# Retention and a gated convolution in one kernel: the first four phases in another order

## The chip, the cores and the metric

The kernel runs on one core of one Trainium2 chip. The metric is the time of one execution on the device, in microseconds; the median of five runs before the change is 165.16 us (164.12 to 170.69).

## What is computed

Eight batches of 576 tokens with eight heads of 64. Retention is attention without a softmax: scores are scaled, multiplied by a decay `gamma_h ** (i - j)` for `i >= j` and by zero otherwise, and multiplied with the values. Its output, 512 features per token, goes through a causal convolution over five tokens (one weight per feature and tap) whose sigmoid gates a linear layer, and through a second linear layer.

```python
scores = (1 / sqrt(64)) * q @ k.T                      # per batch and head
gamma  = 1 - 2.0 ** (-5 - arange(8))
ret    = (scores * where(rel >= 0, gamma ** rel, 0)) @ v
x      = ret.transpose(0, 2, 1, 3).reshape(8, 576, 512)
gate   = sigmoid(sum(conv_w[k] * shift(x, 4 - k) for k in range(5)))
out    = (gate * (x @ w_val)) @ w_out
```

## The kernel before, in words

**Chunks.** A sequence of 576 tokens is cut into two chunks of 256 and a tail of 64. The tails of four batches make one chunk. So there are 18 chunks m (the list `dcs`), worked off in the loop `for m in range(1, ND + 1)` (L507), with chunk 0 done in the straight code ahead of it. Round m works on chunk m's retention, on chunk m−1's convolution and values, and on projections of chunks further back. Engines take their instructions in the order in which the program issues them, since the schedule is written by hand; what an instruction waits for follows from the tiles that it reads and writes.

**Loads.** SP's queue loads k, q and v in float32, chunk by chunk (`load`, L98), the first chunk whole, later ones in two halves each. After chunk 2 comes `w_val` (1 MB), after chunk 3 `w_out` (1 MB, four pieces).

**Casts.** `cast_k`, `cast_q` make bfloat16 tiles `kb` and `qb`, each in two halves (`kb<-fk`, L224), and `cast_v` multiplies the values with the decay `gin` (L238). They run on GpSimd (POOL), except the first keys, which VectorE (DVE) casts.

**Retention of one chunk.** The keys and the queries are turned by TensorE (PE), eight transposes each (`turn`, L260), and copied out of PSUM to `kq` (`take_turned`, L268, ScalarE unless said otherwise). The target of a turn is `tps`, a pool of one bank, unless a bank of the pool `g` is passed. `scores` (L250, `s<-kq`) has two parts, r = 0 and 1, each followed by two `masks` on VectorE (L291). `values` (L305) multiplies the masked scores with the values, `carried` (L305, `o<-kq,sd`) adds what earlier tokens bring through the state. The state of a batch is accumulated in PSUM by `update(m, 0)` and `update(m, 1)` (`st<-vb,kb`), and after each half ScalarE copies it (`take_state`, L375, `sd` or `sl`); the next half writes the same bank and so waits for that copy. `take_x` (VectorE, L340) scales the result by `gout` into `x`.

**Gated layer.** `conv` (L250, `g<-x,dg`) runs the five taps as matmuls with diagonal weights `dg`, in two lists `lo` and `hi` of ten steps of two matmuls each, one list for each of two PSUM banks of the pool `g`. `gate` (ScalarE, L404) takes the sigmoid and frees a bank; `value` (L411) multiplies with `wvb`, the cast of `w_val`, and VectorE makes `z` (L414). `project` (L421) multiplies with `wob`, the cast of `w_out`; ScalarE copies the result (L429, `ob`) and SP stores it.

**Start.** ScalarE computes the tables of decay factors `gout` (four Exps of 128x576) and `gin`, then loads Sigmoid's table by a small activation (L464). VectorE and POOL make the diagonals (`prep_diagonals`, L209). `keep_warm(n)` issues n matmuls on zeros (L446), 128x512 each, which only keep TensorE active.

**Order in the rounds up to m = 3** (`late = m < 4`): eight steps of `lo` and `hi`, `update(m, 0)` between the last steps of `hi`, the state's copy, `update(m, 1)` between the last steps of `lo`, the copy, then `carried(m, 1)` and `scores(m, 1)`. Then keys of chunk m+1 are turned, except that round 2 does so after its two `value` calls; then come `value` and `project` calls by a small table, casts of chunk m+2, `values(m)`, `take_x(m)`, the turn of the queries (round 1 does it before `values`), and a second table of `value` and `project` calls.

Of the kernel before, what the change touches and what calls it, by code (L numbers as in the profile page):

```python
# [13 lines left out]
F32 = mybir.dt.float32  # L14
# [7 lines left out]
def kernel(  # L22
# [58 lines left out]
    with tc.manual_schedule():  # L81
# [45 lines left out]
        def prep_wo(copy, part):  # L127
            copy(wob[:, 2 * part:2 * part + 2], wof[:, 2 * part:2 * part + 2])


        zeros = consts.tile([P, DM], BF16, name="zeros")
        nc.vector.memset(zeros, 0.0)
        ident = consts.tile([P, P], BF16, name="ident")
        nc.gpsimd.memset(ident, 1.0)
        nc.gpsimd.affine_select(ident, ident, pattern=[[-1, P]], base=0, channel_multiplier=1,
# [47 lines left out]
                                lrow.unsqueeze(1).unsqueeze(3).to_broadcast([P, NCH + 1, H, R]), op=ALU.mult)  # L183

        gout = consts.tile([P, NP, S], F32, name="gout")
        for pr in range(NP):
            nc.scalar.activation(gout[:, pr, :], posi, AF.Exp, bias=lsc, scale=lcol[:, pr:pr + 1])
            if pr == 1:
                nc.scalar.activation(gin, gin, AF.Exp)
        warm = consts.tile([P, 1], F32, name="warm")  # L190

        xg = [[xp.tile([P, GB, NP, PAD + (W if c < NCH else TAIL)], BF16, name=f"x{g}{c}") for c in range(NCH + 1)]
              for g in range(B // GB)]
# [14 lines left out]
        def prep_diagonals(o, eng, ones=None):  # L208
            eng.tensor_tensor(dg[:, o], cw[:, :, o].unsqueeze(2).to_broadcast([P, KC, HP]),  # L209
                              (id2 if ones is None else ones).unsqueeze(1).to_broadcast([P, KC, HP]), op=ALU.mult)  # L210
# [16 lines left out]
        def cast_k(m, *copies):  # L227
            cast("k", m, copies)

        def cast_q(m, *copies):  # L230
            cast("q", m, copies)
# [10 lines left out]
        def run(*lists):  # L242

            for k in range(max(map(len, lists), default=0)):
                for group in lists:
                    for f in group[k] if k < len(group) else []:
                        f()
# [6 lines left out]
        def turn(which, m, bank=None):  # L254

            src = (kbf, qbf)[which][m]
            dst = new_bank() if bank is None else bank
            for pr in range(NP):
                for r in range(R):
                    nc.tensor.transpose(dst[:, pr, r, :], src[:, pr, r, :, :].rearrange("p i d -> p (i d)"), ident)  # L260
            return dst

        def take_turned(which, m, bank, *copies):
            if m not in kq:
                kq[m] = tp_sb.tile([P, 2, NP, R, P], BF16, name="kq", bufs=2)
            o = 0
            for (copy, n) in copies or ((nc.scalar.copy, NP),):
                copy(kq[m][:, which, o:o + n], bank[:, o:o + n])  # L268
                o += n
            assert o == NP  # L270
# [86 lines left out]
        def update(m, ab):  # L357
            if m >= ND or dcs[m][0] != "full":
                return []
            kind, b, c = dcs[m]  # L360
            if b not in st:
                st[b] = ps_st.tile([P, NP, D], F32, name="st")
            return [[mm(st[b][half[i], pr, :], lhsT=kbf[m][half[ab], pr, r, i, :],
                        rhs=vbf[m][half[ab], head(pr, i), r, :],
                        start=(c == 0 and ab == 0 and pr == 0 and r == 0), stop=(c == NCH - 1 and ab == 1 and r == R - 1))
                     for r in range(R) for i in range(2)] for pr in range(NP)]
# [74 lines left out]
        def keep_warm(n, t=None):  # L441

            if t is None:
                t = ps_o.tile([P, NP, R, HP], F32, name="o0").rearrange("p o r n -> p (o r n)")
            for _ in range(n):
                nc.tensor.matmul(t, zeros[:, 0:P], zeros, start=True, stop=True)  # L446
# [4 lines left out]
        ones = ps_st.tile([P, NP, D], F32, name="st")[:, 0, :]  # L451
        nc.tensor.matmul(ones, ident, idb, start=True, stop=True)
        keep_warm(6)
        cast_k(0, (v_copy, 0), (v_copy, 1))
        prep_diagonals(0, nc.gpsimd)
        bank = turn(0, 0)
        take_turned(0, 0, bank, (v_copy, 4))
        cast_q(0)
        for o in range(1, NP):
            prep_diagonals(o, nc.vector, ones)  # L460
        keep_warm(1)
        bank = turn(1, 0, spare(ps_g, "g", [P, NP, R, P], BF16))
        take_turned(1, 0, bank)
        nc.scalar.activation(warm, lsc, AF.Sigmoid)  # L464
        cast_v(0)
        for (name, f) in (("k", cast_k), ("q", cast_q), ("v", cast_v)):
            f(1)
        keep_warm(2)
        run(scores(0, 0))
        masks(0, 0, 0)  # L470
# [1 line left out]
        run(scores(0, 1, spare=True))  # L472
        masks(0, 1, 0)
        masks(0, 1, 1)
        keep_warm(2)
        run(update(0, 0))
        take_state(0, 0)
        run(update(0, 1))
        take_state(0, 1)
        keep_warm(2)  # L480
        run(carried(0, 1))
        bank = turn(0, 1)
        take_turned(0, 1, bank, (s_copy, 1), (s_copy, 3))
        keep_warm(1)

        nc.tensor.matmul(spare(ps_g, "g")[:, 0:P], zeros[:, 0:P], kq[1][:, 0, 0, 0, :], start=True, stop=True)
        run(*values(0, 1))
# [8 lines left out]
        pass_on(0)  # L496
        cast_v(2)
        prep_wv(g_copy, 1)
        keep_warm(4, spare(ps_g, "g"))
        run(scores(1, 0))  # L500
        masks(1, 0, 0)
        masks(1, 0, 1)
# [4 lines left out]
        for m in range(1, ND + 1):  # L507
            now, nxt, last = ok(m), ok(m + 1), m == ND
            late = m < 4
            hi, lo = conv(m - 1)  # L510

            if now and m > 1:
                run(scores(m, 0))
                masks(m, 0, 0)
                masks(m, 0, 1)
            if last:
                run(lo, hi)
                gate(m - 1, 1)
                gate(m - 1, 0)
            elif late:  # L520
                run(lo[0:8], hi[0:8])
                run(pairs(update(m, 0)), hi[8:10])
                take_state(m, 0)
                gate(m - 1, 0)
                run(pairs(update(m, 1)), lo[8:10])
                take_state(m, 1)
                gate(m - 1, 1)
                run(carried(m, 1))
            else:
                run(carried(m, 1))  # L530
                run(pairs(update(m, 1)), lo[0:2])
                take_state(m, 1)
                run(lo[2:10], hi[0:8])
                gate(m - 1, 1)
                run(pairs(update(m + 1, 0)), hi[8:10])
                take_state(m + 1, 0)
                gate(m - 1, 0)
            if now:
                run(scores(m, 1))
                masks(m, 1, 0)  # L540
                masks(m, 1, 1)

            if last:
                value(m - 1, 1, spare(ps_s, "s1"))
                value(m - 1, 0, spare(ps_s, "s0"))
                project(m - 2, 0)
                project(m - 2, 1)
                project(m - 1, 0, last=True)
                project(m - 1, 1, last=True)
                continue  # L550
            def turn_keys():
                if nxt:
                    bank = turn(0, m + 1)
                    take_turned(0, m + 1, bank)

            def turn_queries():
                if nxt:
                    bank = turn(1, m + 1, spare(ps_g, "g", [P, NP, R, P], BF16) if m == 1 else None)
                    take_turned(1, m + 1, bank)

            if m != 2:
                turn_keys()
            if m == 1:
                turn_queries()
                keep_warm(4, spare(ps_g, "g"))

            if m == 2:
                prep_wv(s_copy, 0)
            for (f, n, i) in {1: (), 2: ((value, 0, 1), (value, 0, 0)),
                              3: ((value, 2, 1), (project, 0, 0), (project, 0, 1))}.get(  # L570
                                  m, ((value, m - 1, 1), (project, m - 2, 0))):
                f(n, i)
            if m == 2:
                turn_keys()
            if m == 2:
                prep_wo(g_copy, 1)
            if ok(m + 2):
                cast_k(m + 2)
                cast_q(m + 2)
                cast_v(m + 2)  # L580

            run(*values(m, 1))
            run(*values(m, 0))
            run(carried(m, 0))
            take_x(m, 0)
            take_x(m, 1)
            pass_on(m)

            if m > 1:
                turn_queries()  # L590
            if m == 1:
                keep_warm(2, spare(ps_g, "g"))
            if m == 2:
                prep_wo(s_copy, 0)
            for (f, n, i) in {1: (), 2: ((value, 1, 1), (value, 1, 0)),
                              3: ((value, 2, 0), (project, 1, 0), (project, 1, 1))}.get(
                                  m, ((value, m - 1, 0), (project, m - 2, 1))):
                f(n, i)
            for name in "kqv":
                if ok(m + 2 + LB):  # L600
                    load(name, m + 2 + LB)
            if m == 3:
                run(update(m + 1, 0))
                take_state(m + 1, 0)
# [28 lines left out]
```

## Time and profile before

| | |
|---|---|
| median of five runs | 165.16 us |
| profiled execution, whole | 164.12 us |
| its span in the profile | 162.4 us |
| ScalarE (ACT) busy | 93.2 us, 57% |
| POOL busy | 82.2 us, 51% |
| mean DMA rate over the span | 248 GB/s, 40.36 MB |

A row of the timeline reads: start and busy time in us, engine, line, operation, output <- inputs, how many, and in brackets how long the engine stood idle before it and what released it. PEld is the loading of weights, which overlaps matmuls. Matmuls of one row overlap, so the sum of their durations is more than the row's time. The ends of matmuls are modelled.

The rounds begin, by the start of their main run of convolution matmuls, at 16.16, 22.73, 32.77, 43.71 and 52.27 us (m = 1 to 5).

### The profile page before, as it was taken

To read this page: it belongs to the slowest core of one execution; us is meant where nothing else is said; L and a number is where in the kernel's file an instruction comes from. 1 tells how busy PE (TensorE), PEld (TensorE's weight loads), DVE (VectorE), ACT (ScalarE), POOL (GpSimd) and SP (SyncE) were. 2 spreads that over 40 slices of the span, in tenths; PEclk is the share of its full clock that TensorE was granted. 3 is DMA by queue.
4 is the path that set the end of the run, shared out by engine and by line. 5 is a ranking of instruction groups with operands and counts; after the bars stand their busy time and mean duration, and the time that the engine had idled before them with its cause. 6 is when DMAs were issued, how large, how long until landed. Compare 5 with 4: busy or idle time off the path is not lost.

```text
span 162.4 us, 7764 instructions
## 1 busy us (share of the span) xinstructions
PE 147.3 (91%) x3391; PEld 105.9 (65%) x3391; DVE 100.3 (62%) x186; ACT 93.2 (57%) x151; POOL 82.2 (51%) x120
## 2 busy tenths in 40 slices
PE   6978877889989999999899999998999999999970
PEld 2435756776566777777577868775777777765720
DVE  6783665765548586775467767675766767766210
ACT  3875636755564757665566657574657576652340
POOL 4597767478845432557566848364746155000000
PEclk9999999999999999999999999999999999999997
DMA  4999999999998568999999997999894777121134
GB/s 123 346 346 343 384 304 253 305 316 311 347 342 251 158 147 196 277 330 319 339 336 307 316 300 224 264 316 321 253 296 122 177 178 263 40 97 66 68 129 129
DMA packets 69729, 40.36 MB, mean 248 GB/s; under 512 B 14891, under 2 KB 64063, under 8 KB 69695
## 3 DMA queue, kind: packets, MB, share of 16 engines
q1 hardware_dynamic: 69504, 39.59, 82.0%
q8 instruction: 26, 0.43, 1.1%
q10 hardware_dynamic: 190, 0.27, 0.6%
q14 instruction: 9, 0.07, 0.1%
HBM read 30.42 MB, written 9.44 MB: 245 GB/s over the span
## 4 chain that ended last, share of the span: by engine, by line
PE 83%; ACT 6%; DMA 3%; issue 3%; DVE 1%; POOL 1%; ACTq 0%; SPq 0%
PE g L421 19%; PE g L411 18%; PE g L250 14%; PE tps L260 11%; PE o L305 8%; PE s L250 6%; PE st L250 4%; DMA fqe<-in_q_dram 3%; ACT kq L268 2%; ACT sd L375 1%; PE s L411 1%; ACT ob L429 1%; PE g L260 1%; POOL qb L224 1%; ACT gate L404 1%
## 5 line engine op out<-in xcount | busy, mean ns | idle before, releaser
L291 DVE TENSOR_TENSOR p<-s,mask 128x512 bf16<-128x512 f32 x62 | 39.9, 685 | 19.9 <-PE s L250 19.9
L268 ACT COPY kq<-tps 128x1024 bf16<-128x1024 bf16 (+2 forms) x33 | 32.6, 992 | 14.5 <-PE tps L260 14.2
L411 PE MATMUL g<-x,wvb 128*128 128x256 bf16 x272 | 35.3, 273 | 1.5 <-ACT wvb L215 0.7
L421 PE MATMUL g<-wob,z 128*128 128x512 bf16 x144 | 36.4, 379 | 0.0
L238 POOL TENSOR_TENSOR vb<-fv,gin 128x1024 bf16<-128x1024 f32 x15 | 28.5, 1902 | 12.9 <-DMA fv<-in_v_dram 12.9
L429 ACT COPY ob<-g 128x512 f32<-128x512 f32 x34 | 19.9, 586 | 25.6 <-PE g L421 24.5
L250 PE MATMUL g<-x,dg 64*64 64x256 bf16 x720 | 30.8, 272 | 1.5 <-DVE x L340 0.6
L340 DVE TENSOR_TENSOR x<-o,gout 128x512 bf16<-128x512 f32 x32 | 22.2, 745 | 15.2 <-PE o L305 15.2
L411 PEld LDWEIGHTS <-wvb 128*128 128x128 bf16 x288 | 26.6, 98 | 4.8 <-issue 1.1
L414 DVE TENSOR_TENSOR z<-gate,g 128x512 bf16<-128x512 f32 x34 | 23.4, 687 | 9.1 <-PE g L411 8.2
L404 ACT ACTIVATE gate<-g 128x512 f32<-128x512 f32 x36 | 21.3, 603 | 10.7 <-DVE p L291 5.4
L250 PEld LDWEIGHTS <-dg 64*64 64x64 bf16 x720 | 23.1, 105 | 4.4 <-issue 2.8
L224 POOL CAST kb<-fk 128x512 bf16<-128x512 f32 x30 | 17.6, 615 | 7.7 <-DMA fk<-in_k_dram 5.6
L421 PEld LDWEIGHTS <-z 128*128 128x128 bf16 x144 | 14.1, 98 | 10.6 <-issue 0.5
L224 POOL CAST qb<-fq 128x512 bf16<-128x512 f32 x30 | 17.6, 616 | 6.5 <-DMA fq<-in_q_dram 4.5
L250 PE MATMUL s<-kq 64*64 64x128 bf16 (+1 forms) x560 | 15.8, 217 | 1.2 <-ACT kq L268 0.9
L250 PEld LDWEIGHTS <-kq 64*64 64x64 bf16 x576 | 11.4, 106 | 8.3 <-issue 7.8
L353 POOL COPY x<-x 128x16 bf16<-128x16 bf16 x16 | 3.2, 197 | 24.6 <-DVE x L340 24.6
L250 PE MATMUL st<-vb,kb 64*64 64x64 bf16 x512 | 13.6, 193 | 1.9 <-ACT sd L375 1.8
L250 PEld LDWEIGHTS <-kb 64*64 64x64 bf16 x512 | 12.0, 109 | 3.5 <-issue 3.5
L305 PEld LDWEIGHTS <-vb 64*64 64x64 bf16 x576 | 8.5, 107 | 8.4 <-issue 8.3
L375 ACT CAST sd<-st 128x256 bf16<-128x256 f32 x24 | 8.9, 370 | 7.8 <-PE g L250 6.2
(75 smaller groups left out, 132.1 us busy)
## 6 DMA issues: line engine op xcount, KB each, us to landing
out_dram<-ob SPq DMA_DIRECT2D x32, 256.0 KB, 4.2
fk<-in_k_dram SPq DMA_DIRECT2D x26, 256.0 KB, 4.9
fq<-in_q_dram SPq DMA_DIRECT2D x26, 256.0 KB, 4.9
fv<-in_v_dram SPq DMA_DIRECT2D x26, 256.0 KB, 5.1
fke<-in_k_dram SPq DMA_DIRECT2D x4, 256.0 KB, 4.5
fqe<-in_q_dram SPq DMA_DIRECT2D x4, 256.0 KB, 4.5
fve<-in_v_dram SPq DMA_DIRECT2D x4, 256.0 KB, 5.1
wvf<-in_moe_w_val_dram SPq DMA_DIRECT2D x1, 1024.0 KB
```

The costliest lines, as they stand in the source:

```text
L224: copy(dst[:, i], src[:, :, 1:3] if i else src[:, :, 0::3])
L238: eng.tensor_tensor(vbf[m][:, h:h + n], loaded["v", m][:, h:h + n], g[:, h:h + n].unsqueeze(3).to_broadcast([P, n, R, D]), op=ALU.mult)
L250: return lambda: nc.tensor.matmul(*a, skip_group_check=True, **kw)
L268: copy(kq[m][:, which, o:o + n], bank[:, o:o + n])
L291: nc.vector.tensor_tensor(p[:, :, 0:n], sps[m, r][i][:, :, 0:n], mask[dcs[m][0], r].unsqueeze(1).to_broadcast([P, NP, n]), op=ALU.mult)
L305: nc.tensor.matmul(o, start=key not in opened, stop=False, skip_group_check=True, **kw)
L340: nc.vector.tensor_tensor(xg[b // GB][c][:, b % GB, :, x0:x0 + P].rearrange("p o (n r) -> p o r n", r=R), ops[m, ab], gout[:, :, t0:t0 + P ...
L404: nc.scalar.activation(t, gps[n][i], AF.Sigmoid)
L411: nc.tensor.matmul(vps[:, j, :], lhsT=wvb[:, o, 2 * i + j, :], rhs=xs(n, slice(0, P), o, PAD), start=(j == 0 and o == 0), stop=(j == 1 and ...
L414: nc.vector.tensor_tensor(z, gsb[n][i], vps, op=ALU.mult)
L421: nc.tensor.matmul(o, lhsT=zsb[n, j // 2][:, j % 2, i * P:(i + 1) * P], rhs=wob[:, j, :], start=(j == 0), stop=(j == NP - 1))
L429: nc.scalar.copy(ob, o)
```

## The change

It touches the start and rounds 1 to 3; from round 4 on each engine gets the same instructions in the same order.

At the start, a small Exp on ScalarE (`warm`) is issued as soon as the zeros exist. The four `gout` activations become calls placed one by one. ScalarE takes half of the casts of k0, q0 and k1. The turned queries of chunk 0 are copied by VectorE, and one block of diagonals goes from VectorE to POOL. Two of the calls of `keep_warm` go and four change their count: 28 matmuls on zeros become 21.

In round 1, `carried(1, 1)` and `scores(1, 1)` come before `update(1, 1)`, and the queries of chunk 2 are turned after `values(1)`. In rounds 2 and 3 `update(m, 0)` comes after three steps of each list and `update(m, 1)` at the end, with the rest of the convolution between them; the order of the two gates is turned around. In round 3 both `value(2, ·)` stand together, the cast of half of `w_out` on ScalarE moves there from round 2, and the keys of chunk 4 are turned after `project(0, ·)`, directly before the queries.

```diff
+        warm = consts.tile([P, 1], F32, name="warm")
+        nc.scalar.activation(warm, zeros[:, 0:1], AF.Exp)
...
-        for pr in range(NP):
+
+        def prep_gout(pr):
             nc.scalar.activation(gout[:, pr, :], posi, AF.Exp, bias=lsc, scale=lcol[:, pr:pr + 1])
-            if pr == 1:
-                nc.scalar.activation(gin, gin, AF.Exp)
-        warm = consts.tile([P, 1], F32, name="warm")
+
+        prep_gout(0)
+        nc.scalar.activation(gin, gin, AF.Exp)
+        prep_gout(1)
...
-        cast_k(0, (v_copy, 0), (v_copy, 1))
+        cast_k(0, (v_copy, 0), (s_copy, 1))
         prep_diagonals(0, nc.gpsimd)
+        prep_gout(2)
         bank = turn(0, 0)
+        prep_diagonals(1, nc.vector, ones)
         take_turned(0, 0, bank, (v_copy, 4))
-        cast_q(0)
-        for o in range(1, NP):
-            prep_diagonals(o, nc.vector, ones)
+        cast_q(0, (g_copy, 0), (s_copy, 1))
+        prep_gout(3)
+        nc.scalar.activation(warm, lsc, AF.Sigmoid)
+        prep_diagonals(3, nc.gpsimd)
+        prep_diagonals(2, nc.vector, ones)
         keep_warm(1)
         bank = turn(1, 0, spare(ps_g, "g", [P, NP, R, P], BF16))
-        take_turned(1, 0, bank)
-        nc.scalar.activation(warm, lsc, AF.Sigmoid)
+        take_turned(1, 0, bank, (v_copy, 4))
         cast_v(0)
-        for (name, f) in (("k", cast_k), ("q", cast_q), ("v", cast_v)):
-            f(1)
+        cast_k(1, (s_copy, 0), (g_copy, 1))
+        cast_q(1)
+        cast_v(1)
         keep_warm(2)
...
-        keep_warm(2)
+        keep_warm(1)
         run(update(0, 0))
         take_state(0, 0)
         run(update(0, 1))
         take_state(0, 1)
-        keep_warm(2)
         run(carried(0, 1))
         bank = turn(0, 1)
         take_turned(0, 1, bank, (s_copy, 1), (s_copy, 3))
-        keep_warm(1)
...
-        keep_warm(4, spare(ps_g, "g"))
+        keep_warm(2, spare(ps_g, "g"))
...
             elif late:
-                run(lo[0:8], hi[0:8])
-                run(pairs(update(m, 0)), hi[8:10])
+                n = 8 if m == 1 else 3
+                run(lo[0:n], hi[0:n])
+                run(pairs(update(m, 0)), lo[n:n + 2])
                 take_state(m, 0)
+                run(lo[n + 2:10], hi[n:8])
+                gate(m - 1, 1)
+                if m > 1:
+                    run(pairs(update(m, 1)), hi[8:10])
+                    take_state(m, 1)
+                else:
+                    run(hi[8:10])
                 gate(m - 1, 0)
-                run(pairs(update(m, 1)), lo[8:10])
-                take_state(m, 1)
-                gate(m - 1, 1)
                 run(carried(m, 1))
...
                 masks(m, 1, 1)
+            if m == 1:
+                run(pairs(update(m, 1)))
+                take_state(m, 1)
...
-            if m != 2:
+            if m not in (2, 3):
                 turn_keys()
             if m == 1:
-                turn_queries()
-                keep_warm(4, spare(ps_g, "g"))
+                keep_warm(2, spare(ps_g, "g"))
...
-                              3: ((value, 2, 1), (project, 0, 0), (project, 0, 1))}.get(
+                              3: ((value, 2, 1), (value, 2, 0))}.get(
...
-            if m > 1:
-                turn_queries()
+            if m == 3:
+                prep_wo(s_copy, 0)
+                project(0, 0)
+                project(0, 1)
+                turn_keys()
+            turn_queries()
             if m == 1:
-                keep_warm(2, spare(ps_g, "g"))
-            if m == 2:
-                prep_wo(s_copy, 0)
+                keep_warm(3, spare(ps_g, "g"))
...
-                              3: ((value, 2, 0), (project, 1, 0), (project, 1, 1))}.get(
+                              3: ((project, 1, 0), (project, 1, 1))}.get(
```

## The prediction

> **What bounds the kernel now.** I read the page's table of engines first, then its slices, then the waits of the first phases, then the timeline around each wait.
>
> ```profile
> PE 147.3 (91%) x3391; PEld 105.9 (65%) x3391; DVE 100.3 (62%) x186; ACT 93.2 (57%) x151; POOL 82.2 (51%) x120
> ...
> PE   6978877889989999999899999998999999999970
> ...
> PE 83%; ACT 6%; DMA 3%; issue 3%; DVE 1%; POOL 1%; ACTq 0%; SPq 0%
> ```
>
> TensorE binds: 91% of the span and 83% of the chain. But the slices (4.06 us each) show where it is not full: up to 36 us they stand at 6 to 8, later at 9. The change works in that stretch only. Busy time by stretch says how much is there: from 8.9 to 42.4 us TensorE is busy 28.9 of 33.5 us, so 4.6 us are idle, and 4.25 us of the busy time are matmuls on zeros (line 446), which fill waits. More than that sum, 8.9 us, cannot be won. From 51.2 to 150 us it is busy 96.5 of 98.8 us with nothing of the change in it: what the early phases win arrives at the end as it is.
>
> Who ends TensorE's waits there, from the view of waits for 8.9 to 43.5 us (us in total, times, longest):
>
> ```profile
> PE st L250 <- ACT sd L375: 1.8, 4, 0.5
> PE s L250 <- ACT kq L268: 0.9, 2, 0.7
> PE g L411 <- ACT wvb L215: 0.7, 1, 0.7
> PE g L250 <- DVE x L340: 0.6, 1, 0.6
> PE tps L260 <- ACT kq L268: 0.5, 1, 0.5
> ```
>
> It is ScalarE, not a load, that TensorE waits for: the second half of a state update behind the copy of the state, scores behind the copy of turned keys and queries. The timeline has the pieces (start us, us, engine):
>
> ```profile
> 2.81 1.28 ACT L187 ACT_TABLE_LOAD   x1 [2.81 <-DVE tok L164]
> 8.10 1.01 ACT L268 COPY kq<-g 128x1024 bf16<-128x1024 bf16 x1 [0.71 <-PE g L260]
> 9.13 1.28 ACT L464 ACT_TABLE_LOAD   x1
> 14.68 1.03 PE L446 MATMUL g<-zeros 128*128 128x512 bf16 x4
> 24.09 0.37 ACT L375 CAST sd<-st 128x256 bf16<-128x256 f32 x1 [2.80 <-PE g L250]
> 24.51 0.22 PE L250 MATMUL st<-vb,kb 64*64 64x64 bf16 x3 [0.45 <-ACT sd L375]
> 28.58 1.01 ACT L268 COPY kq<-tps 128x1024 bf16<-128x1024 bf16 x1 [1.64 <-PE tps L260]
> 29.64 0.61 PE L260 MATMUL tps<-ident,qb 128*128 128x128 bf16 x8 [0.47 <-ACT kq L268]
> ```
>
> The last two rows matter most later: one bank serves keys and queries, so the queries of a chunk are turned only once ScalarE has emptied the bank, 1.01 us after it begins.
>
> [...] the first Exp starts at 4.11, 0.02 us after the load ended. [...] at 29.10 one load of qb went ahead, its matmul stood until 29.64. So a waiting turn holds all matmuls behind it. [...] Here the first ten zero matmuls run about 0.43 us apart, the four at 14.68 about 0.217. [...]
>
> **Part by part.** I replay the program order of the changed kernel in the rows' durations; loads land as before.
>
> Start, to the first scores (9.16). ScalarE loads Exp's table at about 1.45, after issuing its load of conv_w, and not at 2.81. But the exp of gin must wait for VectorE's product (4.35 to 4.55), so only one gout (0.81) comes before it: gin 4.57 to 4.8, gout to 5.57, then half of the first key cast. Its cost on ScalarE is not shown; nearest rows are wvb (0.62) and ob (0.59); bounds 0.5 to 0.7, I take 0.6. The keys are ready at 6.15; two VectorE casts made it 5.97, so 0.15 worse. Queries: POOL's half lands at 6.8, ScalarE's follows a third gout (6.1 to 6.9) and ends 7.5; before 7.38. The copy of the turned queries goes to VectorE (0.69 by its row, against 1.01): 8.2 to 8.9. Scores at 8.95, so −0.2. One diagonal goes to POOL (0.91) between its half of q and the values' load, which lands at 7.84: it ends at 7.75, hidden by that wait; without that cover it costs 0.9.
>
> First chunk, to scores(1,0) (15.94). The Sigmoid table load now runs 8.25 to 9.53 and is followed by half of k1's cast (to 10.35). The first state copy then starts at 10.35, not 10.75: −0.4. Two zero matmuls between update(0,1) and carried go (0.54), one more before the turn's copy: carried 11.2 (12.08), turn of k1 to 11.9, its first copy 12.35 (13.34), masks ready 11.95. Values 12.4, turn of q1 to 13.75 (q1's cast still ends by 12.03), copy to 14.85. Scores(1,0) at 14.9: −1.04 in all. Two of four zero matmuls behind it go and gain nothing: copy kq ends the wait.
>
> m = 1, to conv(1) (22.73). The state wait stays (0.35 of 0.45, four matmuls are put into it), but carried and scores(1,1) come ahead of update(1,1): masks end 18.75 (20.06), values 18.8 (20.52), x done 20.95 (22.68). That would be −1.7. However, the queries of chunk 2 are now turned after the values: turn 19.5 to 20.1, ScalarE's copy to 21.15, scores(2,0) in front of the convolution. Conv(1) at 21.45: −1.28. The new wait is the copy, 0.45 us beyond the zero matmuls; conv(1) and all behind it queue there.
>
> m = 2, to conv(2) (32.77). update(2,1) starts behind 22 matmuls of the convolution (28 ns each, 0.6 us), which cover the state copy (0.04+0.37+0.05): −0.46. ScalarE is next late: state copy 23.8, gate 24.3, two wvb casts (1.14) to 25.4, where value(0,0) stood at 26.99. It waits 1.0 where it waited 0.7, so of 0.46 about 0.3 arrives: −1.6. The wait of the turn of q3 (0.47) stays. POOL's order is unchanged. Conv(2) at 31.2: −1.57.
>
> m = 3, to the end of project(1,1) (42.48). The state wait (0.43) is covered again: −2.0. value(2,0) comes up beside value(2,1), so its product waits for VectorE's masks (1.29), covered by the two values and values(3). The wob cast (1.05) moves from 31.20 to about 33.9 and ends at 34.95, before project(0,0) at 35.6. The turn of k4 leaves its place among other work and stands right before the turn of q4, in the one bank: turn to 38.05, ScalarE's copy (its ob copies are done by 38.1) to 39.1, then the turn of q4. **New wait, 1.05 us**, with both turns' matmuls and four products' worth of projections queued behind it; in the kernel before, 3.4 us of work stood between. project(1,1) ends at 41.5: −1.0.
>
> SP: the loads keep their order, and early loads go out without waiting for compute; the first four output stores come about 1 us earlier at most. From m = 4 the instruction order is the same.
>
> Sum of the stages: −0.2 −0.84 −0.24 −0.29 −0.43 = −2.0, and +1.05 for the new wait: about −1.0 us. The profiled execution took 164.12 (span 162.4 and 1.72 around it), so it would be 163.1. That run was the lowest of five; the median is 165.16, so I forecast **164.2**, −0.6%. A measurement of this kernel can tell about 1%, 1.65 us, from no change.
>
> **Rivals.** (a) The sum and its unknowns, −0.3 to −1.65: 163.5 to 164.9. The unknown ScalarE cast (±0.1, twice) and the chain's pauses shown as "issue" (four of 0.5 to 0.72, with no releaser, which may fall elsewhere) make its width. Chance 0.5.
>
> (b) The pair of turns costs little, or the waits that zero matmuls hide are shorter than I take them: without the new wait −2.05, 163.1; with one "issue" pause halved too (−0.25) 162.9. For it: TensorE has up to 8.9 us to give. Against it: only one bank, and the 0.47 wait at 29.64 shows the mechanism. Chance 0.28.
>
> (c) The change does not speed what it says, since loads bind: DMA is full until 48 us and POOL waits for v1, q2, wvf, v3. Against: before, v1's cast ended 14.27 and is wanted at 15.9, q2's 17.88 at 19.5, wvf's 21.93 at 23.5, v3's 27.97 at 31.6; 1.5 us of slack everywhere. If the replay misses that slack, 165.2. Chance 0.12.
>
> (d) **Slower**: seven of 15 zero matmuls are gone between 9.7 and 21.8 us, and TensorE idles there some 0.5 us at a time. [...] Against: the same stretch has idle pieces of 0.67 now and stays at full clock. Chance 0.10.
>
> **Numbers.** Adding the spread of the runs (median against lowest, 1.0) to the better end of (b), 162.9−1.0, [...] 161.9 to 166.4 leaves out about 0.2. Faster by over 1%: (b) and a share of (a) that spread carries over, 0.36. Slower by over 1%: most of (d) and some of (c), 0.10. Same: 0.54.
>
> **What would show it.** Right: scores(1,0) near 14.9; conv(1) near 21.4 right behind a kq copy; no wait of st on sd at m = 2 and 3; at m = 3 a wait of about 1.05 us of the turn of q4 on ScalarE's kq copy; conv(3) about 1 us earlier. Wrong: that wait missing or above 1.5, zero matmuls 0.43 apart after 9 us, POOL casts that end TensorE's waits, or a TensorE share from 51 us on that differs from before.

## The result and the profile after

The changed kernel takes 163.72 us (median of 43 runs, 162.04 to 167.53), the kernel before, run beside it, 164.74 us (80 runs, 161.69 to 170.69). The ratio is **1.0005 [0.9982, 1.0028]**: no change that can be measured. It takes from each kernel only the runs within 1.5% of its fastest, so it says nothing of the 1.0 us between the two medians, and of profiles well above that limit no length is compared below (before's, at 164.12, lies on it). The profiled execution took 163.84 us, its span is 162.1; before it was 164.12 and 162.4.

From the page of the changed kernel: TensorE's busy time, its slices, the queue that carries instructions, and the shares of the chain that ended last.

```profile
PE 146.1 (90%) x3384; PEld 105.9 (65%) x3384; DVE 99.8 (62%) x185; ACT 94.0 (58%) x154; POOL 82.3 (51%) x119
...
PE   6868968797899999998999999997999999999970
...
q8 instruction: 26, 0.43, 1.2%
...
PE 75%; DMA 7%; ACT 7%; issue 3%; SPq 2%; POOL 2%; DVE 1%; ACTq 0%; DVEq 0%; POOLq 0%
```

TensorE is 1.2 us less busy, about what the seven zero matmuls took (0.217 each, 1.5), and it is 0.9 us more idle (16.0 us of its span, before 15.1). DMA now stands in the chain with 7%, where it had 3%.

Who ends TensorE's waits from 8.5 to 43.5 us (total, times, longest):

```profile
PE tps L264 <- ACT kq L272: 1.6, 2, 1.2
...
PE s L254 <- ACT kq L272: 1.1, 2, 0.7
...
PE g L254 <- issue: 1.0, 1, 1.0
...
PE st L254 <- ACT sd L379: 0.5, 1, 0.5
```

The waits for the copied state have gone from 1.8 us in four places to 0.5 in one. A turn behind the copy `kq` now costs 1.6 instead of 0.5. And a wait of 1.0 with no releaser ("issue") holds the convolution.

TensorE's timeline of the same kernel shows where:

```profile
14.72 0.42 PE L254 MATMUL s<-kq 64*64 64x128 bf16 x16 [0.67 <-ACT kq L272]
21.14 0.42 PE L254 MATMUL s<-kq 64*64 64x128 bf16 x16 [0.45 <-ACT kq L272]
21.36 0.38 PE L254 MATMUL g<-x,dg 64*64 64x256 bf16 x5
22.75 0.41 PE L254 MATMUL g<-x,dg 64*64 64x256 bf16 x7 [1.01 <-issue]
...
40.68 0.61 PE L264 MATMUL tps<-ident,qb 128*128 128x128 bf16 x8 [1.16 <-ACT kq L272]
41.12 1.89 PE L425 MATMUL g<-wob,z 128*128 128x512 bf16 x8
...
75.72 0.22 PE L254 MATMUL st<-vb,kb 64*64 64x64 bf16 x3 [0.46 <-POOL vb L242]
```

Conv(1) begins at 21.36, 1.37 us earlier than before (22.73), runs five matmuls, and stops until 22.75. Without the stop its sixth matmul would have come at about 21.50, so the stop costs some 1.25 us: nearly all that had been won is gone there.

| us | before | after | won so far | forecast |
|---|---|---|---|---|
| scores(0,0) | 9.16 | 8.90 | 0.26 | 0.2 |
| scores(1,0) | 15.94 | 14.72 | 1.22 | 1.04 |
| conv(1) begins | 22.73 | 21.36 | 1.37 | 1.28 |
| conv(1) past its pause | – | 22.75 | about 0.1 | – |
| conv(2) begins | 32.77 | 32.47 | 0.30 | 1.57 |
| project(1,1) ends | 42.48 | 43.02 | −0.54 | 1.0 |

From 45 to 150 us both kernels issue the same. One row of windows for each kernel (stretch, its length, busy time and count of PE, PEld, DVE, ACT, POOL, granted clock, DMA share, GB/s), before first:

```profile
45.00:150.00 105.00, 102.22 (x2492) 76.24 (x2483) 70.99 (x110) 63.45 (x104) 50.25 (x68) 1.00 0.81 240
```

```profile
45.00:150.00 105.00, 102.76 (x2520) 76.75 (x2511) 71.13 (x110) 64.07 (x104) 50.72 (x68) 1.00 0.82 241
```

Even here 2.2 to 2.8 of 105 us are idle. These idle pieces turned out to matter as much as the edited stretch.

### The profile page after: what moved, and what is told of

It reads as the page before. It is cut to its first block, busy times and chain, and to the rows that moved or that the text cites. A ratio compares the mean times of both kernels' runs of the same rounds, so it can differ in the third digit from the quotient of the medians.

```text
span 162.1 us, 7761 instructions
## 1 busy us (share of the span) xinstructions
PE 146.1 (90%) x3384; PEld 105.9 (65%) x3384; DVE 99.8 (62%) x185; ACT 94.0 (58%) x154; POOL 82.3 (51%) x119
## 4 chain that ended last, share of the span: by engine, by line
PE 75%; DMA 7%; ACT 7%; issue 3%; SPq 2%; POOL 2%; DVE 1%; ACTq 0%; DVEq 0%; POOLq 0%
PE g L425 17%; PE g L415 17%; PE g L254 13%; PE tps L264 10%; PE o L309 7%; PE s L254 5%; DMA fv<-in_v_dram 4%; PE st L254 3%; DMA fqe<-in_q_dram 3%; ACT kq L272 3%; SPq L90 2%; ACT ob L433 1%; POOL vb L242 1%; PE s L415 1%; PE g L264 1%
## 5 line engine op out<-in xcount | busy, mean ns | idle before, releaser
L254 PE MATMUL g<-x,dg 64*64 64x256 bf16 x720 | 31.7, 272 | 2.2 <-issue 1.4
L418 DVE TENSOR_TENSOR z<-gate,g 128x512 bf16<-128x512 f32 x34 | 23.4, 687 | 9.1 <-PE g L415 8.4
L254 PE MATMUL st<-vb,kb 64*64 64x64 bf16 x512 | 14.1, 193 | 0.9 <-ACT sd L379 0.5
L254 PEld LDWEIGHTS <-kb 64*64 64x64 bf16 x512 | 12.8, 109 | 2.1 <-issue 1.9
L309 PE MATMUL o<-p,vb 64*64 64x128 bf16 (+1 forms) x576 | 11.4, 216 | 0.0
```

The lines of the kernel that those rows point to most:

```text
L254: return lambda: nc.tensor.matmul(*a, skip_group_check=True, **kw)
L309: nc.tensor.matmul(o, start=key not in opened, stop=False, skip_group_check=True, **kw)
L418: nc.vector.tensor_tensor(z, gsb[n][i], vps, op=ALU.mult)
```

## Experiments

### What the pause is

The pauses have no releaser, but a pattern. I counted TensorE's weight loads from the start (about one in every two of its instructions) and set each pause beside the packets of the queue called "instruction" in the trace. It moves 26 packets of 16,384 bytes, and 7761 instructions of all engines include 6768 of TensorE's (3384 loads and as many matmuls), or about 26 times 260.

| kernel | pause (us) | weight loads before it | rest by 128 | packet landed | landing to end |
|---|---|---|---|---|---|
| before | 45.91–46.69 | 863 | 95 | 45.36 | 1.33 |
| before | 109.66–110.45 | 2396 | 92 | 108.99 | 1.46 |
| after | 21.39–22.75 | 350 | 94 | 21.48 | 1.27 |
| after | 83.05–83.69 | 1756 | 92 | 82.32 | 1.37 |
| after | 109.44–110.69 | 2394 | 90 | 109.34 | 1.35 |

The five rests lie within 90 to 95, so the pauses stand whole multiples of 128 pairs, 256 instructions, apart, give or take 5 pairs; and beside each stands one packet. So I take such a pause for a fetch of TensorE's program. After the landing of the packet TensorE still takes about 1.3 us to go on (1.27 to 1.46 in the table), and a packet takes 0.88 to 2.09 us by its record in these two profiles. In the kernel before a packet landed at 20.88 us too; conv(1) was then waiting for `x` until 22.68, which covered it. Conv(1) earlier has no such cover.

**Moving the block's edge.** A block is the 256 instructions from one such place in TensorE's program to the next, and the edge is that place. Small matmuls take the place of zero matmuls at the start (`pad(n)` issues n of them, 64x64 by 64 columns, on zeros), so that 64, 128 or 192 more of TensorE's instructions (rows) stand ahead of conv(1). 128 rows, `pad` itself left out:

```diff
-        keep_warm(4)
+        pad(48)
...
-        keep_warm(6)
+        pad(21)
+        keep_warm(5)
```

> Changed kernel; the first four matmuls on zeros are 36 small ones (64x64 by 64 columns), so that all later TensorE instructions stand 64 rows (32 weight loads, 32 matmuls) later in the program; nothing else differs. Theory F (the pause of 1.01 us inside conv(1), which no wait explains, is TensorE's program running out until the next block of 256 instructions, 16 KB, has been fetched by a DMA): the pause leaves the sixth matmul of conv(1), which is matmul 349 of the program in the changed kernel; a pause, if there is one, again stands at matmul 349 of the new count, which is now the turn of q2, and pauses later in the program also stay at the same count (1755, 2394) and so fall on other work. Rival D (a wait for data that the profile hides): the pause stays at the sixth matmul of conv(1), at count 381. For the time F says only that it moves, by up to 1.5 us either way; D says that it stays within 0.3 us of the changed kernel.

> As the run with 64 rows, with 128 rows (64 weight loads, 64 matmuls) more than the changed kernel; 69 small matmuls and five large ones stand in place of the ten at the start. F: no pause at the sixth matmul of conv(1); the block's edge is at matmul 349 of the new count, which falls on values(1), and the next at 477, which falls on the end of round 2's first part; pauses at counts that are 93 (give or take 2) modulo 128. D: the pause stays at the sixth matmul of conv(1). Time: F another one than the changed kernel's by up to 1.5 us either way, D within 0.3 us.

> As the run with 64 rows, with 192 rows (96 weight loads, 96 matmuls) more than the changed kernel; 102 small matmuls and four large ones stand in place of the ten at the start. F: no pause at the sixth matmul of conv(1); the block's edge at matmul 349 falls on scores(1, 1); pauses at counts that are 93 (give or take 2) modulo 128. D: the pause stays at the sixth matmul of conv(1). Time: F another one than the changed kernel's by up to 1.5 us either way, D within 0.3 us. If the many small matmuls make the turn of k0 late, that shows before 7 us and is taken off.

64 rows gave 163.71 us, 1.0001 [0.997, 1.0032]; 128 rows 163.75, 0.997 [0.9915, 1.0024]; 192 rows 165.46, 1.0076 [1.0033, 1.0119]. The timeline with 64 rows:

```profile
21.32 0.42 PE L254 MATMUL s<-kq 64*64 64x128 bf16 x16 [0.46 <-ACT kq L272]
21.54 0.53 PE L254 MATMUL g<-x,dg 64*64 64x256 bf16 x12
```

and with 128:

```profile
21.47 0.53 PE L254 MATMUL g<-x,dg 64*64 64x256 bf16 x12
...
23.95 0.19 PE L254 MATMUL st<-vb,kb 64*64 64x64 bf16 x1 [0.62 <-issue]
```

Conv(1)'s twelve matmuls run through in all three kernels (the third at 23.75), so the pause does not belong to the convolution or its data. With 128 rows it stands at 23.13–23.95, at weight load 478, which is 350 and one block further. With 64 rows pauses stand at weight loads 1117 and 2522 (55.57–56.55 and 115.00–116.70), with 192 at 989 and 2395: the rest by 128 is 90 to 93 in all of them. So the pause belongs to a count in TensorE's program and not to the work that stands there. Moving it did not make the kernels faster, since pauses fall elsewhere instead. The 192 rows lost 2.4 us at the start, where the many small matmuls hold up the turn of k0 (scores(1,0) at 17.11 instead of 14.72), 1.1 us of it in the median beside before's 164.36, so their time, unlike their pauses, says nothing of the edge.

### The new wait of round 3

The keys of chunk 4 are turned before the projections, and the projections again stand between the two turns of the one bank:

```diff
             if m == 3:
                 prep_wo(s_copy, 0)
+                turn_keys()
                 project(0, 0)
                 project(0, 1)
-                turn_keys()
             turn_queries()
```

> Changed kernel, but in round 3 the keys of chunk 4 are turned before project(0, 0) and project(0, 1) instead of after them; the same instructions otherwise. Theory T (the two turns in one bank cost what the wait shows, 1.16 us): the wait of the turn of q4 on ScalarE's copy is gone or under 0.2 us, the long run of conv(3) matmuls starts near 43.1 instead of 44.25, and the time falls by about 1.1 us against the changed kernel, a ratio to the kernel before of about 0.993. Rival: the gain is taken back in rounds 4 and 5 by another wait (copies of projections, loads), and the ratio stays within 0.998 to 1.003.

163.47 us (22 runs) beside 164.36 of before: **0.9932 [0.9895, 0.9969]**, faster than both kernels. TensorE's timeline:

```profile
21.36 0.38 PE L254 MATMUL g<-x,dg 64*64 64x256 bf16 x5
21.93 0.41 PE L254 MATMUL g<-x,dg 64*64 64x256 bf16 x7 [0.19 <-issue]
...
36.35 0.62 PE L264 MATMUL tps<-ident,kb 128*128 128x128 bf16 x8
36.80 1.89 PE L425 MATMUL g<-wob,z 128*128 128x512 bf16 x7
38.53 0.61 PE L264 MATMUL tps<-ident,qb 128*128 128x128 bf16 x8
```

The turn of the queries waits for nothing. It also shows how loose a pause is: up to conv(1) the program is that of the changed kernel, yet the packet landed at 20.66, not 21.48, and the pause ended at 21.93. Conv(3)'s main run came 2.15 us earlier than in the changed kernel (42.10 against 44.25), 1.16 of it the wait and 0.82 the pause; the span ended 0.9 earlier. Most of the rest went again at 81.18–83.55, where the changed kernel stood from 83.05 to 83.69: keys first came to that edge 1.87 us earlier, but the block's packet landed only 0.24 earlier (82.08 against 82.32).

```profile
83.55 0.27 PE L254 MATMUL g<-x,dg 64*64 64x256 bf16 x1 [2.10 <-issue]
```

### The parts of the change alone

Start alone: the code of the changed kernel ahead of the loop, the loop of before. Rounds alone: the reverse.

> The kernel before with the change's start alone (everything ahead of the loop over rounds); rounds 1 to 3 as before. Theory F+T (the start is worth 1.2 us where scores(1, 0) begin, the pauses for fetched instructions and the two adjacent turns took it back): scores(1, 0) at 14.7 as in the changed kernel, conv(1) 0.5 to 1.3 us ahead of 22.73 as a pause falls or not, no wait of the turn of q4, a ratio of 0.994 to 0.998. Rival A (later rounds absorb any gain of the start, loads above all): conv(3) is ahead of 43.71 by 0.5 us or more, and the ratio still lies within 0.999 to 1.002.

> The kernel before with the change's rounds 1 to 3 alone; the start, with all its matmuls on zeros up to scores(1, 0), as before. Theory F+T: scores(1, 0) at 15.9; the covered state waits give 0.5 to 0.9 us, the adjacent turns of round 3 cost 1.1 to 1.2 us, so conv(3) is 0 to 0.7 us later than 43.71 and the ratio is 1.000 to 1.005. Rival A: a ratio within 0.999 to 1.001, since what is late here is caught up later.

Start alone 164.27 us, 0.999 [0.9947, 1.0033]; rounds alone 164.01, 0.9965 [0.9921, 1.0008]. Neither can be told from no change nor from a gain of half a per cent. The rounds alone were expected at 1.000 to 1.005 and came out lower, a miss. The rounds' profile has the turn's wait (1.2 us), the start's has not. In the start's profile (one run, the fastest of 14) conv(3) began 0.82 us ahead of before (42.89 against 43.71), so a gain that is there at the end of the edited stretch did not show in the ratio: that is the rival of its expectation.

### Are the loads the bound?

In the changed kernel POOL got v of a later chunk at 73.67 and made `vb` from it until 75.66; TensorE waited 0.46 for it. Before, the same cast ended at 75.09 and was used at 75.44. So I had each round issue its loads of chunk m+4 ahead of the stores on SP's queue (right behind `pass_on(m)` and not at the end of the round), with the keys first and in the kernel before:

```diff
+            for name in "kqv":
+                if ok(m + 2 + LB):
+                    load(name, m + 2 + LB)
...
-            for name in "kqv":
-                if ok(m + 2 + LB):
-                    load(name, m + 2 + LB)
```

> The run with the keys first, and in each round the loads of chunk m + 4 are issued ahead of the stores of that round's second projections instead of behind them. Theory A (once the early rounds are faster, TensorE waits around 73 to 77 us for values whose load stood behind a store in SP's queue): no wait of update on POOL's vb is left in the middle rounds, and the ratio falls from 0.993 to about 0.989. Rival B (it is the rate of the DMA engines that makes these loads late, not when they are issued): waits on vb stay or grow and the ratio stays at 0.992 to 0.995.

> The kernel before, with the loads of chunk m + 4 issued ahead of the stores of that round's second projections. Theory A: TensorE does not wait for loads in the kernel before, so nothing is won, a ratio of 0.998 to 1.002. Rival B': hidden waits for loads are there too and the ratio falls below 0.996; or the burst of earlier loads delays stores and instruction fetches and it rises above 1.003.

A miss. Keys first with early loads took 165.55 us, 1.0138 [1.0076, 1.02]; before with early loads 163.71, 0.9973 [0.9934, 1.0012]. The waits of the former, over the span, on all engines:

```profile
ACT ob L433 <- DMA out_dram<-ob: 3.7, 2, 3.0
...
PE g L254 <- ACT ob L433: 2.4, 2, 2.1
```

TensorE's wait for `vb` shrinks to 0.2, but the stores now stand behind the loads on SP's queue, ScalarE's copy `ob` waits for a store (3.0 us once), and a bank of the convolution waits for that copy (2.1). In the kernel before the same edit cost nothing that can be measured; why it did no harm there is not shown.

**Without the loads.** The last four kernels leave out the loads of k, q and v of chunks 2 to 17 and use the tiles of chunks 0 and 1 instead, so that their output is another one; the work on all engines but the loading stays the same.

```diff
         def load(name, m):
+            if m >= 2:
+                loaded[name, m] = loaded[name, m % 2]
+                return
```

> The kernel before with the loads of chunks 2 to 17 left out: those chunks work on the data of chunks 0 and 1, so the output is another, and all engines but the loads do the same work. Theory G (what spreads the times and takes the early gain back is traffic of the loads: fetches of instructions that come late, values that come late): no unexplained pause above 0.3 us is left on TensorE after 16 us, the runs spread over less than 2 us instead of 5, and the ratio is 0.980 to 0.990. Rival H (the pauses have nothing to do with the loads): pauses of 0.5 to 1.5 us stay and the ratio is above 0.993.

> The changed kernel with the loads of chunks 2 to 17 left out in the same way. G: it is 0.6 to 1.1 us ahead of the kernel before without these loads (1.0 by the sum of the prediction; less by up to 0.4 if covering the state waits wins less), so its ratio is lower by 0.004 to 0.007; conv(1) begins at 21.4 and runs through. Rival S (the new order itself wins nothing): the two differ by less than 0.3 us.

> The run with the keys turned first in round 3, with the loads of chunks 2 to 17 left out in the same way. G: another 1.1 us ahead of the changed kernel without these loads, the whole wait of the turn of q4, a ratio lower by 0.006 to 0.007. Rival: less than 0.4 us.

> The kernel before with the change's start alone, with the loads of chunks 2 to 17 left out in the same way. G: 1.0 to 1.3 us ahead of the kernel before without these loads, as far as scores(1, 0) are ahead (14.7 against 15.9), so about as far as or a little further than the whole change. Rival: the whole change is more than 0.5 us ahead of its start alone.

| without loads of chunks 2–17 | median | range | ratio to before with loads |
|---|---|---|---|
| before | 161.63 | 161.11–163.90 | 0.991 [0.9877, 0.9943] |
| start alone | 159.91 | 159.76–160.09 | 0.9801 [0.9745, 0.9856] |
| changed | 160.33 | 160.11–160.50 | 0.9825 [0.977, 0.988] |
| changed, keys first | 158.97 | 158.62–159.16 | 0.9741 [0.9685, 0.9796] |

Now the parts can be told apart. The change wins 1.3 us (1.0 between the lowest runs), and the forecast sum was 1.0. The start alone wins 1.7 (1.35 between the lowest; 1.0 to 1.3 was expected), the rounds give 0.4 back, and keys first takes off another 1.36 (the forecast price of the wait was 1.05, the trace's 1.16). The windows of the changed kernel without these loads, same stretch and columns as above:

```profile
45.00:150.00 105.00, 104.33 (x2545) 78.59 (x2534) 71.64 (x111) 64.78 (x106) 47.43 (x67) 1.00 0.21 73
```

DMA works at 0.21 instead of 0.82, and TensorE is busy 104.3 of 105 us where it was busy 102.8. From the first gate of round 4 to the end, where the order of instructions is one and the same, the profiles of the last three take 113.9 us each, that of before, the slowest of its 17 runs, 114.2. With the loads, seven profiles take 115.8 (start alone), 116.6 (128 rows), 116.7 (changed), 117.5 (192 rows), 117.6 (before) and 118.0 (keys first, with early loads too). So the loads cost the later rounds 2 to 4 us, in an amount that differs by more than the whole gain, and the runs of a kernel with loads spread over 3 us or more, up to 9, where those of three of the four without spread over about 0.5 or less.

Where these 2 to 4 us go shows when each profile is set beside the changed kernel without loads, one weight load after another, from the first gate of round 4. A kernel falls behind in a few steps only. They stand at edges of the program (a rest by 128 of 90 to 95), or at the one update that waits for `vb`, near 74 to 76 us:

| with loads | behind in all (us) | steps at edges | at `vb` |
|---|---|---|---|
| start alone | 1.84 | 1.34, six | 0.53 |
| changed | 2.75 | 2.05, three | 0.74 |
| before | 3.56 | 3.23, six | – |
| changed, keys first | 4.03 | 3.06, three | 1.02 |

(Before has 0.32 more at 52.27, which it has without the loads too.) The view of waits names no pause of the start alone in this stretch, so steps like these, up to 0.34 us, can escape it.

What was not foreseen: a pause of 0.8 to 1.1 us at 16 to 19 us stays in all four kernels without these loads, while the first loads still run (conv(1) of the changed one begins at 22.0, not at 21.4, and runs through); after 25 us there is none. In the changed kernel:

```profile
17.29 0.30 PE L257 MATMUL g<-x,dg 64*64 64x256 bf16 x3 [0.78 <-issue]
```

## Why the prediction was right, and where it was not

The forecast of 164.2 came true with 163.72; of its reasons some did not. That the number fits is in part luck. The 0.6% that it forecast is not in the ratio, whose interval ends at 0.9982, a gain of 0.2%. The forecast was taken off a median of five runs, 165.16, which over 80 runs is 164.74.

- **Start** and **first chunk**: right, keys at 6.14 (6.15), scores(0,0) at 8.90 (8.95), scores(1,0) at 14.72 (14.9). The cast on ScalarE, taken at 0.6, took 0.60.
- **m = 1**: "Conv(1) at 21.45: −1.28" is right as a beginning (21.36) and wrong as a gain. The failed term is the pause with no releaser, which I let "fall elsewhere" as a width on both sides. It stands at a fixed count of TensorE's program (weight load 350), and a packet of the instruction queue landed 1.27 us before its end; in the profiled run it stopped conv(1) for 1.25 us, which leaves about 0.1 of that gain. Shown by the edge that moved with the rows.
- **m = 2, m = 3**: the waits for the state are gone as said. Of −0.29 about 0.18 arrived (conv(2) is 0.30 ahead, conv(1) behind its pause 0.12), and of −0.43 about 0.25: from the start of conv(2) to the values 2.24 us, against 2.49 to the turn of k4, which stood there before.
- **New wait**, "1.05 us": right in place, cause and size, 1.16, and shown by keys first. Rival (b), that it costs little, is refuted.
- "What the early phases win arrives at the end as it is": **wrong**. It holds without the loads. With them, instruction fetches and v's loads take between 2 and 4 us of the later rounds (the table of steps), in the kernel before as well, and nothing of the gain is left in the ratio. I read the 2.3 idle us of 51.2 to 150 as nothing of the change's; in truth they are the place where a gain can be lost. Rival (c), which lets loads bind, was right in that but put it in the first rounds and on POOL's casts, and there no cast was late.
- Rival (d), half clock: not there. In the changed kernel no zero matmul after 9 us runs slow (0.38 to 0.39 us each, where the slow ones at the start take 0.63). How long such a stretch lasts and what it costs, and with it the upper end of 166.4, was my estimate; no trace of before shows it. The kernel before without loads had such a stretch in its profile (20.2 to 23.4 us, four zero matmuls 0.43 us apart) with every zero matmul in place, so it can come without any of them gone.
- Two readings of the slices were off, and nothing rests on them: the second slice, 4 to 8 us, stands at 9 already, and a few later ones at 8.

What stays open: why the mean with loads is so near zero. Each kernel has one profile. The three with that edge in conv(1) (changed, keys first, and keys first with early loads) show a pause of 0.54 to 1.36 us there; how long each pause and each wait for v is over the runs was not measured, and the two halves of the change could not be told apart with the loads on.

## What to carry to other kernels

In these kernels pauses of TensorE without a releaser came back at the same count of instructions (a rest of 90 to 95 by 128 weight loads), and a packet of the instruction queue landed about 1.3 us before their end. Where such a pause shows, look for that packet, and expect that work pulled ahead of such an edge can run into it, as conv(1) did (1.25 us). Where an early stretch is tightened in a kernel that keeps its DMA queues busy (a share of 0.82 here, from 45 to 150 us), also time it with the loads left out: that tells whether the edit is good, apart from whether the gain reaches the end. And two uses of one PSUM bank want work between them that is as long as the copy that empties it: here 1.01 us for `kq`, with a wait of 1.16 where nothing stood between and none where 1.73 us of projections did.

## What the hardware showed beyond that

- Fetches of the program came at different times in kernels whose code is the same up to there: the same block landed at 20.66, 21.32 and 21.48 us in three kernels (keys first, keys first with early loads, changed), and the pause lasted 0.54, 1.02 and 1.36 us between two weight loads. Each of the three packets took 0.95 us, so they differ by when they began (19.71, 20.37 and 20.53). In the changed kernel without the later loads it began at 18.78, and there was no pause; what sets its beginning was not tested. The longest of all seen was 2.4 us (81.18–83.55 with keys first).
- TensorE fell to half clock in the kernel before without loads, from 20.2 to 23.4 us; the slice of its granted clock from 20.3 to 24.3 us stands at 5 tenths. From 16.2 to 20.2 us it had been idle for 1.13 and 0.40 us; the cause was not tested. Zero matmuls are 0.43 us apart there, against 0.217 at full clock:

```profile
21.62 1.91 PE L449 MATMUL g<-zeros 128*128 128x512 bf16 x4
```
